# One list in place of a planner: the order of all operations in an attention kernel with a mixing and a channel stage

## The chip, the core and the metric

The kernel runs on one core of a Trainium2 chip. The metric is the device time of one execution in microseconds (us), the median of several. The core has five sequences of instructions that run side by side and wait for each other through semaphores: TensorE (PE in the profile, its weight loads apart as PEld), VectorE (DVE), ScalarE (ACT), GpSimd (POOL) and SyncE (SP), which here issues all the transfers between main memory and the core's own memory.

## What is computed

Four batches, eight heads, 768 positions, 64 numbers a head. Each position attends to a window of 16 positions either side and to 24 summaries of blocks of 32 positions (the largest key, the mean value). The attention's result x, 768 x 512 a batch, then goes through two stages:

```python
k_sum = k.reshape(B, H, nb, block, D).max(axis=3)
v_sum = v.reshape(B, H, nb, block, D).mean(axis=3)
scores_l = scale * q @ k.T, masked to |i - j| < 16
scores_s = scale * q @ k_sum.T + log(32)
a = softmax(concatenate([scores_l, scores_s]))
x = a @ concatenate([v, v_sum])              # 4 x 768 x 512
theta = x @ w_theta
zr, zi = x * cos(theta), x * sin(theta)
y = w_tok_r @ zr + w_tok_i @ zi              # 768 x 768 weights, mixing positions
u = x + y
out = u + relu(u @ w_ch)
```

Inputs and outputs are 32-bit floats. The weights arrive as pairs of 32-bit words that are turned into floats on the core.

## The kernel before

The work goes by tiles of 128 queries, 24 in all, six a batch. A tile has: scores on PE (tiles s0 and s1, L691, 32 short products), softmax on DVE (L729) and ACT (L733), transposes on PE (pa, L742), the products with v (pa, L716, here "values"), their division by the row sums (xn, L754 to L763), a turn on PE (t, L772), theta on PE (t, L797 for the first six tiles, L802 later), cosine and sine (w, L811 to L827), z (zh and zb, L837) and its split into a high and a low part (L523, L532). When a tile's z is there, one step of the mix can run on PE (m, L865): a batch has two halves of the columns with six steps each, and a step takes one tile's z and one row block of both mixing weights. The mix is over half of all time on PE. The first batch's first half works on whole floats, the rest on high and low parts (three products for one). The channel stage comes last (L906 to L1000).

Around it: SP loads q, keys (kn), v, vn, and weights (wth for theta, wt for the mix, 12 transfers wtr and wti). The block maxima of the keys are taken on DVE (ks, L614), the block means of v for the first batch on PE (pa from x, L620, x being where vn lands), the windows of the keys are copied on ACT or POOL (k, L684). A weight is turned from words to floats in five steps (f and wt, L575 to L586) and split by a cast (L525) and a subtraction (L532). Tiles named with a buffer (x, v, f, w) have between one and four buffers and a transfer waits until the buffer's last reader has ended; v has four (VB=4), two a tile.

What sets the order: all operations are first collected in a list of objects with a cost for each engine that may run them. `Program.schedule` computes due times, walks four times forward and backward through a plan of the times on every engine, and makes a last pass in which tables of numbers (OFF, HOLD and TILT, by kind and index of an operation) shift ranks, hold operations back and tilt the choice between DVE and POOL. The planner chooses the engine of each operation too. The instructions are then issued in that order, so each engine's queue, SP's among them, runs in it.

Two parts of it matter here. From the eighth tile on (FUSE=7) the values of one tile and the scores of the next are one operation, issued on PE as a row, values first (`products(scores)`, L694 to L704, L709). And a POOL operation that uses the memory port it has in common with DVE waits for the latest DVE operation that by the plan has ended before it (GATE, L1119).

Of the kernel before, what the change touches and what calls it, by code (L numbers as in the profile page):

```python
# [54 lines left out]
OFF = {  # L55
# [160 lines left out]
class Program:  # L216
# [4 lines left out]
    LANDING = 2.2  # L221
# [53 lines left out]
    def forward(self, rank, held=None):  # L275
# [7 lines left out]
        for o in self.ops:  # L283
            o.left, o.ready = o.before, held[o.seq] if held else 0.0
# [903 lines left out]
```

## Time and profile before

| | |
|---|---|
| median of the runs | 465.31 us (3 runs, 465.31 to 466.07) |
| the profiled execution | 469.32 us, of it the span 467.5 us |
| PE busy | 441.8 us, 94% of the span |
| DVE busy | 343.8 us, 74% |
| ACT busy | 286.3 us, 61% |
| POOL busy | 89.1 us, 19% |
| transfers | 55.80 MB, mean 119 GB/s |

The span runs from the first to the last instruction of the profiled execution. In a row of a timeline the idle time ahead of an instruction and what released it stand in brackets. The granted clock (PEclk) is the share of TensorE's full clock in a stretch: 1.00 is 2.4 GHz, 0.50 is 1.2 GHz.

### The profile page before, as it was taken

The page shows a single profiled execution, that of the slowest core. Times are in us where ns is not written, and L with a number is a line of the kernel's source. Part 1 is how long each engine was busy: PE and PEld are TensorE (multiplying, and loading weights), DVE is VectorE, ACT ScalarE, POOL GpSimd, SP SyncE. Part 2 cuts the span into 40 slices and gives each one's busy share as a digit, 9 for nine tenths or more (in the row PEclk, how much of TensorE's full clock was granted, in tenths as well). Part 3 has the DMA queues.
Part 4 walks back from the last instruction along what each step waited for, and adds up shares of the span by engine and source line. Part 5 has one row for each costly group of instructions (what it writes and reads, how often), then busy time and mean ns, then how long its engine had stood idle before and what let it go on. Part 6 is the DMA issues. An engine that isn't in the chain of part 4 may idle for free.

```text
span 467.5 us, 9469 instructions
## 1 busy us (share of the span) xinstructions
PE 441.8 (94%) x3552; PEld 357.7 (77%) x3552; DVE 343.8 (74%) x953; ACT 286.3 (61%) x602; POOL 89.1 (19%) x121
## 2 busy tenths in 40 slices
PE   5598699999989999999999999999999999999997
PEld 0365355566778888888888888888888878899996
DVE  2899689997964667575648667563764379999997
ACT  1799779889956479667647878573852232242531
POOL 1131231333400131121012121212000010243340
PEclk9989889999999999999999999999999999999999
DMA  7999833532445252123052321020000480013324
GB/s 289 374 318 423 214 106 133 167 108 62 125 135 184 81 170 71 52 66 103 5 195 87 96 59 58 5 89 0 2 2 1 142 309 0 1 57 112 119 101 152
DMA packets 25005, 55.80 MB, mean 119 GB/s; under 512 B 2944, under 2 KB 8320, under 8 KB 24960
## 3 DMA queue, kind: packets, MB, share of 16 engines
q1 hardware_dynamic: 24960, 55.20, 35.4%
q8 instruction: 28, 0.46, 0.4%
q14 instruction: 17, 0.14, 0.1%
HBM read 45.75 MB, written 9.44 MB: 118 GB/s over the span
## 4 chain that ended last, share of the span: by engine, by line
PE 64%; DVE 15%; DMA 13%; ACT 3%; SPq 2%; issue 1%; POOL 0%; DVEq 0%; POOLq 0%
PE m L865 29%; PE t L802 10%; PE c L981 6%; PE m L981 5%; DMA v<-vg 5%; PE pa L716 4%; PE s L691 3%; PE pa L742 3%; DMA wt<-wtr 3%; SPq L517 2%; DVE wt L532 2%; DMA x<-vn 2%; PE t L772 2%; DMA f<-vT 1%; DVE cb L906 1%
## 5 line engine op out<-in xcount | busy, mean ns | idle before, releaser
L865 PE MATMUL m<-wt,zh 128*128 128x512 f32 (+1 forms) x768 | 182.4, 362 | 0.8 <-DVE x L884 0.6
L865 PEld LDWEIGHTS m<-wt,zh 128*128 128x128 f32 x768 | 123.5, 189 | 34.0 <-issue 13.5
L865 PE MATMUL m<-wt,zl 128*128 128x512 f32 x336 | 86.8, 339 | 0.0
L733 ACT ACTIVATE e<-e,st 128x118 f32<-128x118 f32 x192 | 59.0, 383 | 2.3 <-DVE st L729 2.1
L865 PEld LDWEIGHTS m<-wt,zl 128*128 128x128 f32 x336 | 51.2, 188 | 7.4
L729 DVE CUSTOM_DVE_ANT_0 e<-s,cs 128x118 f32<-128x118 f32 x192 | 42.1, 274 | 13.1 <-PE s L691 9.1
L802 PE MATMUL t<-wth,xh 128*128 128x512 f32 x144 | 47.6, 412 | 1.1 <-DVE xl L778 1.0
L684 POOL COPY k<-kn 128x188 f32<-128x188 f32 x56 | 18.2, 356 | 108.9 <-PE s L691 72.8
L716 PEld LDWEIGHTS pa<-v,e 118*64 118x64 f32 x768 | 25.3, 141 | 14.0 <-DMA v<-vg 5.7
L746 ACT COPY e<-pa 118x512 f32<-118x512 f32 x40 | 22.8, 586 | 21.3 <-PE pa L742 21.1
L716 PE MATMUL pa<-v,e 118*64 118x65 f32 x768 | 28.8, 228 | 7.1 <-DMA v<-vg 7.1
L814 DVE TENSOR_SCALAR w<-w 128x512 f32<-128x512 f32 x17 | 7.2, 426 | 34.2 <-ACT w L811 34.2
L811 ACT ACTIVATE w<-t,bmagic 128x512 f32<-128x512 f32 x24 | 16.5, 687 | 24.8 <-PE t L802 22.4
L532 POOL TENSOR_TENSOR zl<-zb,zh 128x512 fp32r<-128x512 f32 x9 | 13.1, 1455 | 89.0 <-ACT zh L523 65.2
L691 PE MATMUL s<-k,q 64*64 64x118 f32 x768 | 26.1, 274 | 3.7 <-ACT xl L575 1.7
L733 ACT ACT_TABLE_LOAD x20 | 25.7, 1283 | 5.0 <-DVE st L729 4.7
L742 PEld LDWEIGHTS pa<-cs,e 128*118 128x118 f32 x192 | 23.0, 137 | 6.9 <-ACT e L733 1.6
L802 PE MATMUL t<-wth,xl 128*128 128x512 f32 x72 | 28.3, 393 | 0.0
L742 PE MATMUL pa<-cs,e 128*118 128x128 f32 x192 | 28.2, 275 | 0.0
L691 PEld LDWEIGHTS s<-k,q 64*64 64x64 f32 x768 | 20.5, 136 | 9.0 <-issue 3.1
L826 ACT ACT_TABLE_LOAD x21 | 26.9, 1283 | 0.4
L614 DVE TENSOR_REDUCE ks<-kn 128x48 f32<-128x1536 f32 (+1 forms) x10 | 14.3, 1432 | 15.5 <-DMA kn<-kT 15.4
(166 smaller groups left out, 776.8 us busy)
## 6 DMA issues: line engine op xcount, KB each, us to landing
v<-vg SPq DMA_DIRECT2D x48, 195.0 KB, 3.3
q<-qg SPq DMA_DIRECT2D x24, 256.0 KB, 3.2
kn<-kT SPq DMA_DIRECT2D x6, 798.0 KB, 6.2
wt<-wtr SPq DMA_DIRECT2D x6, 768.0 KB, 11.2
wt<-wti SPq DMA_DIRECT2D x6, 768.0 KB, 12.5
f<-vT SPq DMA_DIRECT2D x12, 384.0 KB, 3.4
cu<-u_scratch SPq DMA_DIRECT2D x8, 384.0 KB, 7.1
out<-cu SPq DMA_DIRECT2D x16, 192.0 KB, 1.9
```

The costliest lines, as they stand in the source:

```text
L532: lambda e: V[e].tensor_tensor(dst(), src(), hi().bitcast(F32), op=ALU.subtract), reads, writes, due, port=BOTH)
L684: lambda e, dst=dst, src=src: (nc.scalar.copy if e == "ACT" else V[e].tensor_copy)(dst(), src()), rd, [(k, key)], due, port=BOTH)
L691: scores = (0.79 if len(parts) == 1 else 2.1, [lambda p=p, g=g, h=h, c=c, kk=kk: nc.tensor.matmul(sc[h].get()[ROW[g], p, c], q.get()[ROW[h ...
L716: mm(2 * 0.433 + scores[0] + (0.2 if scores[0] else 0.0), [lambda n=n, g=g, a=a: nc.tensor.matmul(xa[a].get()[ROW[g], n], turned[a].get()[ ...
L729: op({"DVE": 0.205}, lambda eng, n=n: nc.vector.tensor_tensor_reduce(e()[:, n], sc[n % 2].get()[:, 2 * a + n // 2], mask(m), -SCALE, 3.0e3 ...
L733: op({"ACT": 0.288}, lambda eng, n=n: nc.scalar.activation(e()[:, n], e()[:, n], AF.Exp, bias=st.get()[:, n:n + 1], scale=-1.0), [(st, n)] ...
L742: mm(NH * 0.109, [lambda n=n: nc.tensor.transpose(tp.get()[:NK, n], e()[:, n], ident()) for n in range(NH)], [e_ref, (cs, "ident")], [tp], ...
L746: lambda e: (nc.scalar.copy if e == "ACT" else nc.vector.tensor_copy)(t.get()[:NK], tp.get()[:NK].rearrange("k n q -> k (n q)")), [tp], [t ...
L802: calls = [lambda t=t, xx=xx, k=k, c=c: nc.tensor.matmul(th.get(), xx.get()[:, c], w_th[c].get()[:, k], start=(c == 0 and t == 0), stop=(c ...
L826: nc.scalar.activation(w.get()[:, 0], w.get()[:, 0], AF.Sin, bias=bright.get(), scale=-1.0)
L865: nc.tensor.matmul(acc[th](), zz.get()[:, r, cc], w[:, TT[th]], start=(s == 0 and r == 0 and t == 0 and (th == 0 or c == 0)), stop=(s == N ...
L981: calls = [lambda k=k, t=t, x=x, y=y: nc.tensor.matmul(to.get(), weights[n][x][0]()[:, k, j * P:(j + 1) * P], operands[n].get()[:, y, k], ...
```

## The change

The planner goes. `schedule()` reads the order from a string, ORDER, of 2019 numbers: each is the index of an operation in the collected list, with a letter where more than one engine may run it (a ACT, d DVE, g POOL). The tables OFF, HOLD and TILT and the functions `forward` and `backward` are removed. FUSE is 99, so that no tile has its scores in one operation with the values of another. A POOL operation on the shared port waits for the operation ahead of it in the list that uses the port, if that is one of DVE's. The constants of the old plan's costs (SWITCH, LANDING, LAST, c_dma) change too, but nothing reads a time from them any more. The changed file has 227 lines fewer ahead of the kernel's own code, so L691 of before is L464 of after.

```diff
-OFF = {
-    "": {0: -75.284},
...
-HOLD = {
...
-TILT = {
...
+ORDER = """
+6 8 7 9 10 12 11 13 27g 22 29a 28a 31a 30a 32 1 33 41 42 46 34 14 0 161g 162g 66 16 4 44 45 37 35 67d 43 47 38 48 39 36 68d
...
-    LAST = (dict(PE=0, ACT=0.4283, DVE=0.7305, POOL=0.6962, SP=0), -2.5188, 6.204)
+    LAST = (dict(PE=0.0, ACT=0.42, DVE=1.2, POOL=0.95, SP=0.0), 0.0, 0.0)
...
-    def forward(self, rank, held=None):
...
+    def schedule(self):
+        order = []
+        for word in ORDER.split():
+            o = self.ops[int(word.rstrip("padg"))]
+            o.eng = dict(p="PE", a="ACT", d="DVE", g="POOL").get(word[-1]) or min(o.cost)
             order.append(o)
...
-            A1=13, T1=10, PREP=5, QB=2, VSPE=1, VB=4, KN=2, DIRECT=0, FUSE=7, GATE=1, RELOAD=2, RT=6, RM=6, XA=6, XB=2, ZB=4, ZS=6, EB=3, TAU_A=8.2, TAU_M=4,
+            A1=13, T1=10, PREP=5, QB=2, VSPE=1, VB=4, KN=2, DIRECT=0, FUSE=99, RELOAD=2, RT=6, RM=6, XA=6, XB=2, ZB=4, ZS=6, EB=3, TAU_A=8.2, TAU_M=4,
...
-            mm(*scores, due, mode="block")
+            mm(*scores, due, mode="score")
...
+            if o.eng in o.port:
+                mine = [i for i in traced[n:] if i.engine == units[o.eng]]
+                if o.eng == "POOL" and port:
+                    tc.add_manual_dep(mine[0], port.name, mybir.DependencyInfo(
                         mybir.DependencyClass.Sync, mybir.DependencyReason.DATA), reason="port")
+                port = mine[-1] if o.eng == "DVE" else None
```

What the list does is seen in the order of instructions on an engine. Three places follow; a name ends in the number of its buffer in the program, and x4 is four instructions in a row.

PE at the start of the program, before: the last scores of the first tile, the rest of the block sums of v, the first scores of the second tile (s0_190).

```order
L691 MATMUL s1_133<-k_118,q_96 64x118
L691 MATMUL s0_131<-k_118,q_96 64x118
L691 MATMUL s1_133<-k_118,q_96 64x118
L620 MATMUL pa0_98<-x_83,vt_77 24x512 x2
L691 MATMUL s0_190<-k_118,q_104 64x118
L691 MATMUL s1_192<-k_118,q_104 64x118
L691 MATMUL s0_190<-k_118,q_104 64x118
```

The same place after:

```order
L464 MATMUL s1_96<-k_86,q_88 64x118
L464 MATMUL s0_94<-k_86,q_88 64x118
L464 MATMUL s1_96<-k_86,q_88 64x118
L393 MATMUL pa0_154<-x_123,vt_125 24x512 x6
L515 MATMUL pa1_166<-cs_112,e_117 118x128 x4
L515 MATMUL pa0_182<-cs_112,e_114 118x128 x4
L464 MATMUL s0_190<-k_86,q_175 64x118
L464 MATMUL s1_192<-k_86,q_175 64x118
```

All block sums of v (four of them stood ahead of the first tile's scores) now stand between the first and the second tile's scores, together with the first tile's transposes (pa1_166 and pa0_182).

SP from the fifth weight load of the mix on, before: wt are weight loads, v_177 (the first of these) and v_169 are v of the fourth tile, v_154 is of the fifth.

```order
L517 DMA wt_337<-wtr 128x1536
L517 DMA wt_346<-wti 128x1536
L517 DMA wt_356<-wtr 128x1536
L517 DMA wt_363<-wti 128x1536
L517 DMA wt_391<-wtr 128x1536
L517 DMA wt_416<-wti 128x1536
L517 DMA wt_437<-wtr 128x1536
L517 DMA v_177<-vg 96x520
L517 DMA wt_499<-wti 128x1536
L517 DMA v_154<-vg 96x520
L517 DMA v_169<-vg 96x520
```

The same place after, where v_218 and v_222 are v of the fourth tile and v_177 is of the fifth:

```order
L290 DMA wt_294<-wtr 128x1536
L290 DMA wt_296<-wti 128x1536
L290 DMA q_454<-qg 128x512
L290 DMA v_218<-vg 96x520
L290 DMA v_177<-vg 96x520
L290 DMA v_222<-vg 96x520
L290 DMA q_477<-qg 128x512
L290 DMA wt_479<-wtr 128x1536
L290 DMA v_173<-vg 96x520
L290 DMA wt_482<-wti 128x1536
L290 DMA wt_484<-wtr 128x1536
```

The fourth tile's v now stands behind four weight loads and ahead of the other eight; before, all twelve stood ahead of its second transfer.

DVE ahead of the third tile's z (zh_815), before: conversions of weights (f and wt), w, and two reduces of the second batch's keys (ks).

```order
L614 TENSOR_REDUCE ks_731<-kn_690 128x48
L815 ISA w_711<-t_636,w_711 128x512
L581 TENSOR_SCALAR f_724<-f_724 128x768
L581 TENSOR_SCALAR f_735<-f_735 128x768
L583 SCALAR_TENSOR_TENSOR f_724<-wt_391,f_724 128x768
L583 SCALAR_TENSOR_TENSOR f_735<-wt_416,f_735 128x768
L586 SCALAR_TENSOR_TENSOR wt_808<-wt_391,f_724 128x768
L586 SCALAR_TENSOR_TENSOR wt_808<-wt_416,f_735 128x768
L837 TENSOR_TENSOR zh_815<-xn_573,w_711 128x512
L614 TENSOR_REDUCE ks_731<-kn_770 128x48
L756 RECIPROCAL st_616<-st_616 128x4
```

The same place after, where the third tile's z is zh_795:

```order
L352 TENSOR_SCALAR f_765<-f_765 128x768
L354 TENSOR_SCALAR f_763<-f_763 128x768
L354 TENSOR_SCALAR f_765<-f_765 128x768
L356 SCALAR_TENSOR_TENSOR f_763<-wt_488,f_763 128x768
L356 SCALAR_TENSOR_TENSOR f_765<-wt_490,f_765 128x768
L359 SCALAR_TENSOR_TENSOR wt_793<-wt_488,f_763 128x768
L610 TENSOR_TENSOR zh_795<-xn_518,w_661 128x512
L359 SCALAR_TENSOR_TENSOR wt_793<-wt_490,f_765 128x768
```

The reduces of the second batch's keys are now 14 and 25 rows behind this z.

Over the whole program, PE issues the same products. DVE has 27 instructions fewer, POOL 5 more and heavier ones: of the subtractions that split a mixing weight (L532 wt<-wt) seven go from DVE to POOL. ACT has 16 loads of its function tables fewer. In 18 places PE goes from one tile's scores straight to another's values; before, it went from values straight to scores in 18.

## Rows read from the trace of the kernel before

**Rows 1.** table of stretches: us; busy of PE, PEld, DVE, ACT, POOL; clock, DMA

```profile
0.00:43.40 43.40, 30.47 (x316) 16.66 (x317) 33.13 (x119) 28.91 (x73) 7.78 (x17) 0.96 0.95 345
43.40:60.00 16.60, 12.08 (x67) 7.36 (x66) 12.07 (x33) 12.79 (x34) 4.40 (x5) 0.86 0.81 241
60.00:120.00 60.00, 58.02 (x435) 35.61 (x434) 54.00 (x145) 52.42 (x115) 19.67 (x26) 0.98 0.34 111
120.00:140.00 20.00, 18.62 (x158) 15.47 (x157) 16.09 (x42) 13.72 (x28) 3.76 (x4) 1.00 0.48 152
...
360.00:467.50 107.50, 102.83 (x581) 95.73 (x580) 91.45 (x156) 34.24 (x57) 22.39 (x11) 1.00 0.31 108
```

**Rows 2.** waits of PE: us in all, times, longest us

```profile
PE pa L716 <- DMA v<-vg: 7.1, 3, 4.3
```

**Rows 3.** PE's timeline: start, us, operation, count, idle time before

```profile
5.09 6.51 PE L620 MATMUL pa<-x,vt 128*24 128x512 f32 x8 [5.09 <-DMA x<-vn]
...
25.11 1.85 PE L691 MATMUL s<-k,q 64*64 64x118 f32 x32 [1.10 <-DMA q<-qg]
...
34.76 1.04 PE L691 MATMUL s<-k,q 64*64 64x118 f32 x32
35.73 1.15 PE L716 MATMUL pa<-v,e 118*64 118x65 f32 x32
...
43.42 2.74 PE L865 MATMUL m<-wt,zh 128*128 128x512 f32 x8
...
56.67 2.00 PE L716 MATMUL pa<-v,e 118*64 118x65 f32 x32 [4.33 <-DMA v<-vg]
...
74.71 4.03 PE L865 MATMUL m<-wt,zh 128*128 128x512 f32 x12
```

**Rows 4.** one stretch of the same table, with the half clock

```profile
57.00:59.00 2.00, 2.00 (x33) 1.88 (x30) 0.47 (x3) 0.52 (x3) 0.00 (x0) 0.50 0.03 11
```

**Rows 5.** stretches, with DVE's busy time alone: clock, DMA share

```profile
22.45:42.40 19.95, 19.68 (x82) 0.91 0.99 354
42.40:73.71 31.31, 24.65 (x50) 0.89 0.69 218
```

**Rows 6.** DVE's timeline

```profile
8.28 3.91 DVE L614 TENSOR_REDUCE ks<-kn 128x24 f32<-128x768 f32 x4 [7.34 <-DMA kn<-kT]
...
57.85 0.28 DVE L729 CUSTOM_DVE_ANT_0 e<-s,cs 128x118 f32<-128x118 f32 x1 [3.29 <-PE pa L716]
...
65.37 1.75 DVE L614 TENSOR_REDUCE ks<-kn 128x48 f32<-128x1536 f32 x1 [0.64 <-DMA kn<-kT]
...
73.71 0.69 DVE L837 TENSOR_TENSOR zh<-xn,w 128x512 f32<-128x512 f32 x1 [0.77 <-ACT w L827]
```

**Rows 7.** SP's timeline: issues of transfers

```profile
40.33 4.01 SPq L517 DMA_DIRECT2D v<-vg  x3
```

**Rows 8.** chain of work that ended last: start, us, what

```profile
42.15 14.47 DMA v<-vg
...
462.13 2.10 PE c L981 x12
```

**Rows 9.** DMA issues: KB each, median us to landing

```profile
v<-vg SPq DMA_DIRECT2D x48, 195.0 KB, 3.3
...
wt<-wtr SPq DMA_DIRECT2D x6, 768.0 KB, 11.2
```

**Rows 10.** one stretch of the table, for its DMA share and GB/s

```profile
30.00:55.00 25.00, 20.96 (x187) 12.26 (x186) 23.78 (x73) 24.30 (x56) 7.01 (x8) 1.00 1.02 364
```

**Rows 11.** groups of instructions by line and form: busy, mean ns

```profile
L532 DVE TENSOR_TENSOR wt<-wt 128x768 fp32r<-128x768 f32 x8 | 7.4, 964 | 0.0
...
L532 POOL TENSOR_TENSOR wt<-wt 128x768 fp32r<-128x768 f32 x3 | 6.5, 2167 | 6.5 <-DVE wt L532 5.6 <-ACT w L820 1.0
```

**Rows 12.** timelines of POOL and DVE, one operation of each

```profile
117.20 1.29 POOL L532 TENSOR_TENSOR zl<-zb,zh 128x512 fp32r<-128x512 f32 x1 [1.42 <-ACT zh L523]
...
117.97 1.07 DVE L532 TENSOR_TENSOR zl<-zb,zh 128x512 fp32r<-128x512 f32 x1
```

More of the change, by code (lines that the diff above doesn't have):

```diff
@@ new lines @@
+944 956 892 945 927a 929a 946g 947 969 930 970 1105 894d 895d 1023a 948a 949 978 971 972 973 950 980 1021g 1106a 931a 976
+1107 979 893 1108d 952d 932 933d 1022g 953g 955 957 958 960 975 1020a 977 981 974 984 983 982 985 934a 935 997d 998d 936d
+1109 986 1110 961 1111 988 1112 959 1113 987a 989a 1024 1114d 1011d 1115 990 1052d 991a 1012g 1070a 1178 1025 1033 994d
+1179a 992 1027 995 1026 951 993d 1036 1028 1035 1181d 1180 1031 1029 1030 1001 999 1002 1000 1040 1037 1039 1032 1067g 1069g
+1068g 1009 996d 1034 1038 1003 1005 1182 1041 1183 1018 1134 1136 1019 1065 1064 1004 1043 1013 1184 1014 1185 1116a 1117
@@ new lines @@
+1647 1651 1653 1652 1654 1625 1626 1627 1648 1628d 1649d 1629g 1663 1672 1674 1673 1675 1664d 1650d 1676 1678 1665 1666d
+1667 1668 1670a 1680a 1669 1728 1729 1671g 1735 1741 1730d 1681g 1690a 1742a 1731d 1736d 1732 1737d 1738 1739 1691d 1740
+1733 1743d 1677 1679 1682 1684 1683 1687 1686 1685 1689 1692 1693 1688 1694 1771 1835 1837 1773 1747 1774 1696a 1697g 1748a
+1702a 1734 1757d 1695 1772 1838 1836 1744 1745 1749d 1750 1751 1752 1746 1753d 1775a 1776d 1758d 1765a 1766d 1754d 1703d
+1755d 1756d 1761d 1777d 1698 1700 1699 1701 1793 1759a 1708a 1714a 1794a 1769a 1762d 1770d 1760d 1706 1704 1707 1705 1712
@@ L189 @@
+1926 1930 1937 1870 1802 1898 1895 1806 1887 1810 1877 1874 1934 1834 1827 1951 1947 1958 1813 1866 2001 1988 1976d 1989
+1891 1986 1991 1992 2002a 2004a 2012 1993 1823 1955 1831 2013 2008 2009 2010 2014 2005 1990 1994 2011 2015 2006 2007 2016
+2017 2018 1995 1996 1997
+"""
 class Ref:
@@ L225 @@
               ("block", "whole"): 0.185, ("whole", "split"): -0.06, ("split", "theta"): 0.037, ("theta", "split"): 0.023,
-              ("theta", "whole"): 0.05, ("theta", "block"): 0.12, ("block", "theta"): 0.185, ("whole", "theta"): -0.06}
+              ("theta", "whole"): 0.05, ("theta", "block"): 0.12, ("block", "theta"): 0.185, ("whole", "theta"): -0.06,
+              ("block", "score"): 0.2, ("score", "block"): 0.15, ("score", "split"): 0.185, ("score", "whole"): 0.185, ("score", "theta"): 0.185,
+              ("split", "score"): 0.16, ("whole", "score"): 0.09, ("theta", "score"): 0.12}
     SAME = 0.0
@@ L397, in backward @@
-    def backward(self, span):
-        later = {o: [(u, (self.OWN if o.eng == u.eng and not o.lag else self.LAT[o.eng]) if timed else None) for u, timed in o.users]
-                 for o in self.ops}
-        for refs, _ in self.tags.values():
-            for n, r in enumerate(refs):
-                if n:
-                    later[refs[n - 1].users[0]].append((r.users[0], None))
-                if n >= r.bufs:
-                    for o in refs[n - r.bufs].users:
-                        later[o].append((r.users[0], self.LAT[o.eng]))
-        left, earlier = dict.fromkeys(self.ops, 0), {o: [] for o in self.ops}
-        for o, us in later.items():
-            left[o] = len(us)
-            for u, _ in us:
-                earlier[u].append(o)
-        now = dict.fromkeys(("PE", "ACT", "DVE", "POOL", "SP"), span)
-        ready = {o: span for o in self.ops}
-        heap = {e: [] for e in now}
-        start = {}
-        for o in self.ops:
-            if not left[o]:
-                heap[o.eng].append(o)
-        while len(start) < len(self.ops):
-            best = None
-            for e, os in heap.items():
-                for o in os:
-                    k = (min(now[e], ready[o]), o.done)
-                    if best is None or k > best[0]:
-                        best = (k, o)
-            (end, _), o = best
-            heap[o.eng].remove(o)
-            now[o.eng] = start[o] = end - o.cost[o.eng]
-            for d in earlier[o]:
-                for u, lat in later[d]:
-                    if u is o:
-                        ready[d] = min(ready[d], start[o] + (d.cost[d.eng] if lat is None else -lat - d.lag))
-                left[d] -= 1
-                if not left[d]:
-                    heap[d.eng].append(d)
-        return [start[o] for o in self.ops]
@@ L440, in schedule @@
-    def schedule(self):
-        for o in self.ops:
-            o.before = o.left
-        for o in reversed(self.ops):
-            for u, timed in o.users:
-                o.due = min(o.due, u.due - (0.15 + o.lag if timed else 0.0))
-            o.due -= min(o.cost.values())
-            o.rank += o.due
-        rank = [o.rank for o in self.ops]
-        self.spans = []
-        for n in range(self.ROUNDS):
-            span, order = self.forward(rank)
-            self.spans.append(span)
-            rank = self.backward(span)
-        self.PEN, self.KEEP, self.SAME = self.LAST
-        at = lambda table, o: table.get(o.key[0], {}).get(o.key[1], 0.0)
-        for o in self.ops:
-            o.tilt = at(TILT, o)
-        span, order = self.forward([a + at(OFF, o) for a, o in zip(rank, self.ops)], [at(HOLD, o) for o in self.ops])
-        self.spans.append(span)
+    def schedule(self):
[3 more added lines that the diff above has]
+            o.eng = dict(p="PE", a="ACT", d="DVE", g="POOL").get(word[-1]) or min(o.cost)
+            order.append(o)
+        assert len(order) == len(self.ops)
@@ L484, in c_dma @@
 def c_dma(nbytes, run=2048):
-    return nbytes / run * (7.1 + run / 26.6) * 1e-3 / 16
+    return nbytes / run * (8.4 + run / 22.5) * 1e-3 / 16
 BOTH = ("DVE", "POOL")
@@ L1110, in attn_moe @@
     with tc.manual_schedule(engines={ET.PE, ET.Activation, ET.DVE, ET.Pool, ET.SP}):
-        traced, units = nc.cur_bb.bb.instructions, dict(DVE=ET.DVE, POOL=ET.Pool)
-        shared = []
+        traced, units, port = nc.cur_bb.bb.instructions, dict(DVE=ET.DVE, POOL=ET.Pool), None
         for o in order:
@@ L1115, in attn_moe @@
             o.fn(o.eng)
-            mine = [i for i in traced[n:] if i.engine == units.get(o.eng)]
-            if o.eng == "DVE":
-                shared.append((o.done, mine[-1]))
-            elif o.eng == "POOL" and o.port and K["GATE"]:
-                begin = o.done - o.cost["POOL"]
-                ahead = [i for t, i in shared[-40:] if t + pr.LAT["DVE"] <= begin]
-                if ahead:
-                    tc.add_manual_dep(mine[0], ahead[-1].name, mybir.DependencyInfo(
+            if o.eng in o.port:
+                mine = [i for i in traced[n:] if i.engine == units[o.eng]]
+                if o.eng == "POOL" and port:
+                    tc.add_manual_dep(mine[0], port.name, mybir.DependencyInfo(
                         mybir.DependencyClass.Sync, mybir.DependencyReason.DATA), reason="port")
+                port = mine[-1] if o.eng == "DVE" else None
     es.close()
```

184 lines of the change are left out of this document (66 added, 118 removed), and 123 rows, old and new, of tables (HOLD, OFF, TILT).

## The prediction

> **What bounds the kernel now.** I read the table of stretches first. TensorE (PE) is busy in almost all of the span; what it loses lies at the two ends. Up to the first mix product at 43.4 it works 30.47 of 43.40 us, from there to 60 it works 12.08 of 16.60 at a granted clock of 0.86; from 60 to 120 it idles 1.98, from 120 to 140 1.38, in the last 107.5 us 4.67 [rows 1]. So the end is set by PE's own work plus what it loses, and 17.5 us of its idle time lie ahead of 60. A reordering can win only there; DVE, ACT and POOL work counts only where PE waits for it.
>
> The table of PE's waits names the largest in the head: the values products wait 7.1 us for v, one of these waits 4.3 [rows 2]. In PE's timeline it stands ahead of 56.67, in the middle of the first batch's mix [rows 3]; and then the products run at half clock, 0.50 granted from 57 to 59, after an idle stretch [rows 4]. Why was v late? SP issued it in the group that began at 40.33 [rows 7], behind the weight loads, and the chain shows 14.47 us of transfer from 42.15 on [rows 8]. The DMA engines were full then (share 1.02, 364 GB/s [rows 10]), and a weight load is 768 KB [rows 9], 2.1 us at that rate.
>
> The other side of the head is DVE. Between the second tile's softmax and the first z it is full: 19.68 of 19.95 us; between first and third z it works 24.65 of 31.31 [rows 5]. Of these 6.66 us of waiting 3.29 are the late values product again, seen from DVE; the rest are short ones of which a keys transfer (0.64) and w (0.77) are two [rows 6]. The third z (73.71) is what releases the third mix step at 74.71 [rows 3, 6].
>
> **The change, part by part.** The number of matrix products is the same; the order moves.
>
> *Keys first in SP's queue.* Before, constants and vn stood ahead of the keys, and the key reduces began at 8.28 after 7.34 us of waiting, taking 3.91 [rows 6]. Now the four key transfers stand first. Transfers of vn and constants that were queued ahead of the keys go behind them, so I estimate that the reduces end some 3 us earlier, at 9.2 and not 12.2, and that the first scores begin at about 10. But these scores then come first on PE and cold: the scores at 25.11, released after a wait, took 1.85 and not 1.04 [rows 3], so I take 1.9. Next in PE's order stand all block sums of v (L620, 12 instructions in the trace; eight took 6.51 [rows 3], so 9.8 at that pace and 4.9 if all of it was at half clock; I take 7.8, as they follow cold scores but warm up on the way), then the first tile's transposes (0.9), then the second tile's scores, at about 21. The first softmax comes earlier, but DVE then waits from about 18 to 22 for the second one. I take 22.0 where before had 22.45, the start of the first stretch of [rows 5].
>
> *From there to the first z.* I added up DVE's rows by the mean times of their forms: 19.8 us before between the second softmax and the first z (the trace has 19.95, so the count is good), 22.1 after, as conversions moved ahead. 22.0 + 22.1 + 0.9 for short waits is 45.0 for the first z and 46.0 for the first mix product (42.40 to 43.42 before), 2.6 later. In exchange PE has done about 3.4 us more by then: a values op (1.15 [rows 3]), a theta product of about as much, and twelve transposes.
>
> *The third z.* Between first and third z DVE has 24.0 us of work before (24.65 in the trace) and 21.2 after; the largest piece that leaves is the next batch's key reduce of 1.75 [rows 6]. Without any wait the third z would stand at 66.2. Of the 6.66 us of waits the 3.29 go if v is in time, the key wait goes with the reduce, and 2.7 are left; I keep half, 1.4. That gives 67.6, and the third mix step at 68.6, against 74.71: **6.1 us**. PE itself needs 20.4 us from first mix product to third step by the slots of its instructions (46.0 + 20.4 = 66.4), so DVE ends last there, narrowly. The work done on PE by that point is the same in both orders (49.0 us), so this is a real gain.
>
> *v of the fourth tile.* It holds the above up. Its two transfers now stand ahead of eight weight loads that stood ahead of the second one before: 8 x 768 KB at 364 GB/s is 17 us less in the queue [rows 9, 10]. The last of the two still waits in SP's queue behind a transfer for the fifth tile, whose buffer is free when the third tile's values op has ended, about 36.4 by my count of PE. Issued at 36.8, its bounds are the 3.3 us median of all v transfers [rows 9] and the 14.5 of [rows 8]; with the queue shorter by 17 us I take about the median, so 40 to 41. PE wants it at about 42.4. Behind this wait on SP stand the weight loads of steps three to six; eight of them at 2.1 us land by about 56, and DVE asks for the fifth and sixth of these at 64, so they have cover of some 8 us. Should that cover go, the price is the same DVE path, us for us.
>
> *Steps after that.* POOL takes over seven subtractions of weights (0.964 on DVE, 2.167 on POOL [rows 11]) and some casts; 16 loads of tables go from ACT. Neither engine is late after 120, where PE idles under 1% until the tail; so I count these at what PE loses to them now: at best half of the 1.98, 1.38 and 1.4 of [rows 1] (the last is 4.67 without the 3.3 that stay behind the last product, which ends at 464.2 [rows 8]), at worst as much again for new waits, since the list has longer runs of PE work in batch one. I take a gain of 0.5, bounds -1.5 and +2.5.
>
> *Scores and values as two operations.* Values and scores were one item from the eighth tile on, values first. Now PE has scores first in 18 places, values first in fewer. The only reversed pair in the trace is at 34.76: scores 0.97 to the next start, values 1.15 long [rows 3], nothing beyond the usual. I take 0; bounds 0.1 x 18 = 1.8 either way. The old pairing kept DVE waiting for both; apart, the softmax can begin one op earlier, which matters only where DVE is last.
>
> *The wait of POOL behind DVE.* A POOL operation on the shared port now waits for the DVE operation just ahead in the list, not the last by planned time. Behind it on POOL stand later z remainders and key copies; POOL is idle four fifths of the span in the middle, and a remainder is needed one mix step later. Bounds 0 and one DVE operation (0.7) per remainder that is late; I take 0.
>
> Sum: 6.1 + 0.5 = 6.6 us. The profiled execution took 469.3 (span 467.5 and 1.8 around it), so it would be 462.7; the median of the runs lies 4.0 lower, at 465.31, and as I see no reason why the gain should differ there, **458.7**.
>
> **Rivals.** (a) *DVE waits as much as before.* If something else takes the place of the late v (w from ACT, the transposes), all 6.66 stay: third z 45.0 + 21.2 + 6.7 = 72.9, third step 73.9, gain 0.8 + 0.5 = 1.3: 464.0. For it: DVE's short waits had four different causes. Against: the largest single one has a cause that moves away.
>
> (b) *The port.* At 117.20 a POOL subtraction took 1.29 and DVE's beside it, begun at 117.97, 1.07 [rows 12], where a DVE product of the same size takes 0.69 [rows 6]; so they do delay each other. If the second is stopped for the whole time of the first, seven subtractions of 2.167 cost DVE up to 15.2, less the 6.7 it no longer does: 8.5 us more on DVE. DVE has 6.0 + 3.9 us free from 60 to 140 [rows 1], which covers most of it; one to two us would reach PE: 460.2. The Trainium skill, "SBUF — State Buffer", section "Who interferes with whom", says that a DVE instruction with two SBUF inputs contends with a GpSimd one that reads SBUF, under an exclusive lock in which the second blocks fully. By that rule this rival would be the forecast; the row at 117.97 shows a delay of 0.4, not the full rest of the POOL instruction, so I give it less.
>
> (c) *The fourth tile's v is late again*, the case on the other side. If it takes 14.5 us from 36.8, it lands at 51.3; PE stands from 42.4, and pays some 2.6 for the half clock after it, as at 56.67. From there PE has 22.9 us to the third step: 51.3 + 22.9 + 2.6 = 76.8, 2.1 later than now; less 0.5: 466.9. It turns slower at a landing about 13 us after issue. Against it speak the 17 us less in the queue.
>
> (d) *Better.* The block sums run nearly all at full clock (5.7 and not 7.8) and no short wait is left: first mix at 43.9, third step at 65, gain 9.7, and 2 after it: 453.6.
>
> The change could also not do what its words say: that is the case where the transfers' new times make no difference to the order that the chip sees; it falls together with (a).
>
> **How the numbers follow.** Forecast 458.7: 0.55; (a) 464.0: 0.17; (b) 460.2: 0.08; (c) 466.9: 0.09; (d) 453.6: 0.11. The forecast's own range is 456 to 462, from the bounds of the later steps and of the short waits. The range of 8 in 10 goes from 453.0 to 465.0: it leaves out (c) and the far half of (d). A difference of 0.2% (0.93 us) is about what a measurement of this kernel can tell from no change. Faster than 464.4: forecast, (b), (d) and over half of (a), 0.84; the same: the rest of (a) and a part of (c), 0.08; slower than 466.2: 0.08.
>
> **What would show it.** Right: first scores near 10, first mix product near 46, no wait over 1 us for v ahead of the fourth tile's values, the third step near 68.6, no stretch at half clock after 30, and the same tail. Wrong: a wait for v at 42 to 51 on PE; DVE waiting over 5 us between first and third z; DVE subtractions of z over 1 us beside POOL's in 60 to 140; a first mix product after 48, as the block sums delay the second tile's softmax beyond what I took; or new waits of PE over 3 us after 120.

## The result: 458.76 us after 465.69, and the profile after

The changed kernel takes 458.76 us (median of 4 runs, 457.86 to 459.07), the kernel before beside it 465.69 (4 runs): a ratio of 0.9839, 95% interval 0.9805 to 0.9873, so 1.6% faster. In a later comparison it was 459.59 against 467.21, ratio 0.9812 (0.9760 to 0.9863). The kernel before ran beside every later experiment too, with medians of 467.27, 467.21 and 467.25 us over 70 runs; so the gain is nearer 7.6 us than the 6.9 of the first comparison. The prediction was 458.7. The number was met more closely than the steps behind it deserve; which of them held is the matter of what follows.

The table of stretches of the changed kernel, to be read beside [rows 1] (us; busy time of PE, PEld, DVE, ACT, POOL; granted clock, DMA share, GB/s):

```profile
0.00:46.00 46.00, 33.07 (x366) 19.54 (x367) 35.17 (x125) 30.71 (x77) 10.13 (x24) 1.00 0.98 309
46.00:60.00 14.00, 13.86 (x106) 8.37 (x105) 12.90 (x30) 13.61 (x35) 1.65 (x2) 1.00 0.97 385
60.00:120.00 60.00, 58.48 (x454) 37.93 (x454) 49.94 (x158) 49.34 (x114) 27.57 (x30) 1.00 0.37 108
120.00:140.00 20.00, 19.95 (x167) 17.10 (x166) 12.41 (x36) 11.16 (x29) 6.75 (x6) 1.00 0.42 133
...
360.00:456.70 96.70, 92.36 (x522) 86.72 (x520) 87.68 (x137) 30.68 (x50) 23.31 (x14) 1.00 0.26 94
```

PE idles 13.07 us ahead of 60 (17.45 before), and the granted clock is 1.00 in every stretch of the table (0.96 and 0.86 in the first two before). Busy time went down too, with the same products: 436.5 us and not 441.8.

PE's waits, longest first (us in all, times, longest), where [rows 2] had 7.1 us for v:

```profile
PE s L464 <- POOL k L457: 10.6, 2, 10.0
PE m L638 <- DVE zh L610: 1.5, 2, 1.0
PE m L638 <- DVE x L657: 1.2, 4, 0.5
PE pa L489 <- DMA v<-vg: 0.9, 1, 0.9
```

Of the first row 10.0 us are the start of the program; no other row adds up to more than 1.5. The same in PE's timeline, beside [rows 3]:

```profile
10.03 1.85 PE L464 MATMUL s<-k,q 64*64 64x118 f32 x32 [10.03 <-POOL k L457]
11.81 6.20 PE L393 MATMUL pa<-x,vt 128*24 128x512 f32 x12
...
19.27 1.04 PE L464 MATMUL s<-k,q 64*64 64x118 f32 x32
...
41.42 1.15 PE L489 MATMUL pa<-v,e 118*64 118x65 f32 x30 [0.94 <-DMA v<-vg]
...
44.79 1.45 PE L638 MATMUL m<-wt,zh 128*128 128x512 f32 x4
...
66.07 4.14 PE L638 MATMUL m<-wt,zh 128*128 128x512 f32 x12 [0.50 <-DVE zh L610]
```

First scores at 10.03, the block sums of v behind them, the second tile's scores at 19.27, a wait of 0.94 for the fourth tile's v, the first mix product at 44.79 and the third step at 66.07, which waits 0.50 for DVE. DVE's timeline, beside [rows 6]:

```profile
7.56 2.01 DVE L387 TENSOR_REDUCE ks<-kn 128x24 f32<-128x768 f32 x2 [1.78 <-DMA kn<-kT]
...
20.49 0.28 DVE L502 CUSTOM_DVE_ANT_0 e<-s,cs 128x118 f32<-128x118 f32 x1 [0.31 <-PE s L464]
...
42.85 0.68 DVE L610 TENSOR_TENSOR zh<-xn,w 128x512 f32<-128x512 f32 x1
...
65.33 0.68 DVE L610 TENSOR_TENSOR zh<-xn,w 128x512 f32<-128x512 f32 x1
```

The key reduces end at 9.57, the second softmax begins at 20.49, the first z at 42.85, the third at 65.33. These times move from one execution to the next. A second profile of the changed kernel has, on PE and on DVE:

```profile
11.79 7.48 PE L393 MATMUL pa<-x,vt 128*24 128x512 f32 x12
...
67.47 4.14 PE L638 MATMUL m<-wt,zh 128*128 128x512 f32 x12 [0.54 <-DVE zh L610]
```

```profile
44.11 0.68 DVE L610 TENSOR_TENSOR zh<-xn,w 128x512 f32<-128x512 f32 x1
```

### The profile page after: what moved, and what is told of

It is laid out like the page before. It is cut to its first block, busy times and chain, and to the rows that moved or that the text cites. A ratio compares the mean times of both kernels' runs of the same rounds, so it can differ in the third digit from the quotient of the medians.

```text
span 456.7 us, 9383 instructions
## 1 busy us (share of the span) xinstructions
PE 436.5 (96%) x3552; PEld 355.6 (78%) x3552; DVE 336.3 (74%) x926; ACT 270.8 (59%) x608; POOL 103.0 (23%) x126
## 4 chain that ended last, share of the span: by engine, by line
PE 58%; DVE 12%; issue 1%; ACT 0%; DVEq 0%
PE m L638 31%; PE t L575 9%; PE m L754 4%; PE c L754 4%; PE pa L489 3%; DVE wt L305 3%; PE s L464 3%; PE pa L515 2%; DVE cb L679 2%; PE t L545 2%; DVE x L657 1%; DVE cu L773 1%; PE t L754 1%; DVE zl L305 1%; DVE wth L305 1%
## 5 line engine op out<-in xcount | busy, mean ns | idle before, releaser
L506 ACT ACTIVATE e<-e,st 128x118 f32<-128x118 f32 x192 | 64.0, 388 | 22.7 <-DVE st L502 21.9
L502 DVE CUSTOM_DVE_ANT_0 e<-s,cs 128x118 f32<-128x118 f32 x192 | 45.3, 273 | 4.8 <-PE s L464 4.2
L464 PE MATMUL s<-k,q 64*64 64x118 f32 x768 | 25.9, 273 | 10.7 <-POOL k L457 10.6
L584 ACT ACTIVATE w<-t,bmagic 128x512 f32<-128x512 f32 x24 | 16.5, 686 | 32.2 <-PE t L575 21.4
L464 PEld LDWEIGHTS s<-k,q 64*64 64x64 f32 x768 | 20.4, 136 | 16.5 <-POOL k L457 10.7
L610 DVE TENSOR_TENSOR w<-xn,w 128x512 f32<-128x512 f32 x18 | 12.3, 686 | 20.0 <-ACT w L600 19.9
L457 POOL COPY k<-kn 128x188 f32<-128x188 f32 x40 | 13.0, 347 | 59.9 <-DVE st L529 17.0
L588 DVE CUSTOM_DVE_ANT_0 w<-t,w 128x512 f32<-128x512 f32 x24 | 16.5, 688 | 13.2 <-POOL w L587 12.8
L657 DVE TENSOR_TENSOR x<-m,x 128x512 f32<-128x512 f32 (+1 forms) x32 | 16.3, 549 | 12.7 <-PE m L638 12.7
L575 PEld LDWEIGHTS t<-wth,xh 128*128 128x128 f32 x144 | 22.0, 189 | 2.6 <-DVE xl L551 0.4
L305 POOL TENSOR_TENSOR zl<-zb,zh 128x512 fp32r<-128x512 f32 x9 | 11.8, 1309 | 51.9 <-DVE vs L418 16.5
```

The source lines that it names most:

```text
L305: lambda e: V[e].tensor_tensor(dst(), src(), hi().bitcast(F32), op=ALU.subtract), reads, writes, due, port=BOTH)
L464: scores = (0.79 if len(parts) == 1 else 2.1, [lambda p=p, g=g, h=h, c=c, kk=kk: nc.tensor.matmul(sc[h].get()[ROW[g], p, c], q.get()[ROW[h ...
L502: op({"DVE": 0.205}, lambda eng, n=n: nc.vector.tensor_tensor_reduce(e()[:, n], sc[n % 2].get()[:, 2 * a + n // 2], mask(m), -SCALE, 3.0e3 ...
L506: op({"ACT": 0.288}, lambda eng, n=n: nc.scalar.activation(e()[:, n], e()[:, n], AF.Exp, bias=st.get()[:, n:n + 1], scale=-1.0), [(st, n)] ...
L575: calls = [lambda t=t, xx=xx, k=k, c=c: nc.tensor.matmul(th.get(), xx.get()[:, c], w_th[c].get()[:, k], start=(c == 0 and t == 0), stop=(c ...
L584: op({"ACT": 0.59}, lambda e: nc.scalar.activation(r(), th.get(), AF.Identity, bias=bmagic.get(), scale=1.0 / TWO_PI), [th, bmagic], [R], due)
```

## The experiments

In all experiments but the first the order is written as a list, as in the changed kernel, and only the list is edited; a number is an operation, a letter its engine. Differences in us are taken to the second median of the changed kernel, 459.59; ratios are to the kernel before, run beside each.

### The kernel before a second time, and its order as a list

> The kernel before, unchanged, for a second profile. The profiled execution of before was 4.0 us above the median, and the change's profiled execution is 10.9 us below it while the medians differ by 6.9. Theory A (the late v of the fourth tile and the half clock after it are there in every execution): the second profile shows again a wait of about 4 us for v at 52 to 57 and 0.50 granted after it, and the third mix step near 74.7. Theory B (the late v is a matter of one execution): a wait under 2 us, no half clock from 57 to 62, the third mix step near 71, and the 4 us of difference between profile and median are found there.

Median 468.6 beside 467.27 for the other runs of before, ratio 1.0018 (0.9983 to 1.0052). Its profiled execution took 465.26 (span 463.5). Three lines of its PE timeline:

```profile
23.17 1.78 PE L716 MATMUL pa<-v,e 118*64 118x65 f32 x32 [2.00 <-ACT e L746]
25.58 2.00 PE L691 MATMUL s<-k,q 64*64 64x118 f32 x32 [0.63 <-ACT st L754]
...
71.86 4.03 PE L865 MATMUL m<-wt,zh 128*128 128x512 f32 x12
```

and of its table of stretches:

```profile
24.00:26.00 2.00, 1.37 (x27) 1.21 (x28) 2.00 (x16) 2.00 (x9) 0.91 (x2) 0.50 0.39 131
26.00:28.00 2.00, 2.00 (x35) 1.70 (x31) 2.00 (x6) 2.00 (x8) 0.98 (x1) 0.50 1.01 268
```

The longest wait for v is 2.4 us here and not 4.3, no half clock follows it, and the third step stands at 71.86, 2.85 ahead of [rows 3]. Theory B is right on this execution, but for a wait of 2.4 where it said under 2: of the 4.0 us between the two profiles, 2.85 are there. But against the later medians near 467.2 the first profiled execution lies 2 us above and this one 2 us below. And the late v comes again: a later run, the old list with scores first, has the same order up to the third step, and its PE timeline shows

```profile
57.70 2.00 PE L489 MATMUL pa<-v,e 118*64 118x65 f32 x32 [3.91 <-DMA v<-vg]
...
75.93 4.03 PE L638 MATMUL m<-wt,zh 128*128 128x512 f32 x12
```

with a granted clock of 0.50 from 57 to 61. So a wait near 4 us is there in some executions of the old order and not in others. Half clock there is here all the same, but earlier: from 14 to 16, and from 24 to 30, after 4 us in which PE worked for 2.0 (the wait of 2.00 ahead of 23.17 is one for the eviction of the transposes).

> The changed program with the old order written out as its list: every engine has the instructions of before in the order of before, and only the waits of POOL on the shared port follow the new rule. Theory A (order alone decides): as before, 465.3, between 464.4 and 466.3. Rival (the new port rule itself gives or costs): under 463 or over 468.

```diff
 ORDER = """
-6 8 7 9 10 12 11 13 27g 22 29a 28a ...
+3 0 5 4 14 1 16 6 8 10 12 66 ...
```

Median 468.36, ratio 1.0018 (0.9987 to 1.0049): in us that is above theory A's range and past the rival's 468, but the kernel before beside it was above that range too (467.27), and by the ratio theory A holds. The profiled execution took 465.21, 3.2 us under its median, and the third step stands at 70.62. The new rule of the port does something: POOL's three subtractions of mixing weights take 1825 ns each and not 2167, and POOL is busy for 80.2 us and not 89.1. But no time comes of it that can be measured; what counts is the order.

These profiles give the account on which the rest is built (us; the last column is span less third step):

| profile | span | PE idle | third step at | from there to the end |
|---|---|---|---|---|
| before | 467.5 | 25.71 | 74.71 | 392.8 |
| before, again | 463.5 | 22.52 | 71.86 | 391.6 |
| old order as a list | 463.4 | 24.63 | 70.62 | 392.8 |
| after | 456.7 | 20.23 | 66.07 | 390.6 |
| after, again | 458.4 | 20.77 | 67.47 | 390.9 |

Ahead of the third step PE has done the same products in all of them. The means of the three and of the two: the span falls by 7.2 us, of which 5.6 are there at the third step and 1.6 come later. Split the other way, 3.8 us are less waiting of PE and the other 3.5 are the same products in less time.

More profiles share these heads. The old head of the next section has the third step at 71.17 and the old list with scores first at 75.93; the new head with either seam has it at 65.42 and 65.64. With these there are five profiles of the old head and four of the new one: as means the third step comes at 72.86 and 66.15, 6.7 us earlier. The first z stands at 43.1 and 43.3, so the lead is made behind it, between first and third z: there the old order takes 26.9 to 31.3 us with 24.3 to 24.7 of work on DVE, the new one 21.2 to 22.6 with 21.2 to 21.4.

### Half of one order, half of the other

> The first 450 of the 2019 operations as in the new list (up to the mix steps of the first half of batch one, some 75 us), all others in the order of before. Theory A (the gain is made ahead of the third mix step): 459.5, at most 1.5 us above the changed kernel. Rival C (the gain is made by the rest: values and scores apart, subtractions on POOL, fewer table loads): 464 to 466. The seam itself may cost up to 1.5 us.

```diff
 ORDER = """
 6 8 7 9 10 12 ... 560 509a 692d
-388g 449g 511g 460 ...
+690g 511a 512a 510a ...
```

> The reverse: the first 448 operations as before, the others in the order of the new list. Theory A: 464.5 to 466.5. Rival C: 459 to 460. If both parts give half each, this and the kernel with the new head both stand at 462.

```diff
 ORDER = """
-6 8 7 9 10 12 ...
+3 0 5 4 14 1 ... 436 496 387
...
```

Both missed their ranges: new head 466.92, ratio 0.9991 (0.9964 to 1.0018); old head 467.23, ratio 0.9991 (0.9962 to 1.0020). For the old head the ratio is what theory A said: its third step is at 71.17 and 392.0 us follow, so the new order of the rest gives nothing behind the old head. For the new head it is not: the third step is at 65.42, as early as in the changed kernel, and then 398.3 us follow. So the early third step is the head's work, but in this kernel nothing of it is left at the end. PE's timeline of the kernel with the new head shows where it is lost:

```profile
65.42 4.14 PE L638 MATMUL m<-wt,zh 128*128 128x512 f32 x12 [0.50 <-DVE zh L610]
...
93.43 0.62 PE L515 MATMUL pa<-cs,e 128*118 128x128 f32 x4 [3.41 <-ACT e L506]
...
104.56 0.66 PE L545 MATMUL t<-cs,xn 128*128 128x128 f32 x4 [1.09 <-DVE w L588]
```

The transposes at 93.43 wait 3.41 us for an exponential on ACT; from 60 to 140 PE idles 6.77 us (1.6 in the changed kernel), with a clock of 0.98.

> As the kernel with the new head, but the seam is put at operation 950, about a third into the program, where the two orders have done nearly the same (12 operations differ; 26 at the earlier seam). The earlier one had the third mix step at 65.4 (before: 71.9) and lost it again: PE idles 6.3 us between 60 and 120. Theory A1 (a matter of the seam: the old order hands DVE and ACT work to a stretch that the new head has not prepared): gain kept, ratio to before 0.984 to 0.988, PE idle under 2 from 60 to 120. Rival C1 (the old order of the rest needs the time anyway, and the gain is lost later): ratio 0.995 to 1.000, with the idle time behind the seam.

```diff
 ORDER = """
 6 8 7 9 10 12 ... 929a 946g 947
-969 930 970 1105 ...
+1134 1135 1136 1137 ...
```

464.65 us, ratio 0.9932 (0.9897 to 0.9968), between the two theories. PE idles 1.68 us from 60 to 140, so the loss there was the earlier seam's; a new one stands behind the new seam:

```profile
189.93 1.65 PE L638 MATMUL m<-wt,zh 128*128 128x512 f32 x4 [3.49 <-DVE zh L298]
```

A mix step waits 3.49 us for the high part of z, and the clock is 0.99 over 140 to 360. From 360 to the end PE idles 5.28, in the changed kernel 4.34. The two kernels with the new head stand 7.3 and 5.1 us above the changed kernel; with the later seam the gain of the head is no longer given back ahead of it. How much of the 7.3 and 5.1 is the seam's and how much the old order of the rest needs anyway, these runs don't settle.

> The changed kernel, unchanged, for a second profile and a ratio to before on the same chip as the next three. Ratio to before 0.984 (0.980 to 0.988). In the profile the third mix step near 66 and no stretch at half clock after 12.

459.59, ratio 0.9812 (0.9760 to 0.9863), third step at 67.47 and not 66, no half clock in the table of stretches.

### The transfers: keys first, v of the fourth tile

> The changed kernel with the head of SP's queue as before: constants and two transfers of vn ahead of the keys. PE's order stays, so the first scores still come first. Theory A (DVE is the chain of the head): reduces end near 12.2 and not 9.6, first scores near 13, and most of the 2.6 us stays until the third mix step: 1.5 to 2.6 us slower than the changed kernel, ratio 0.986 to 0.990. Rival (DVE waits for theta's weights at 16 to 19 anyway and catches up): under 1 us slower, ratio 0.981 to 0.985.

```diff
 ORDER = """
-6 8 7 9 10 12 11 13 27g ...
+0 14 1 16 6 8 7 9 10 12 ...
```

462.73 us, ratio 0.9889 (0.9810 to 0.9968): 3.1 slower than the changed kernel, a little over theory A's range. The intervals of the two ratios overlap, but the runs don't: 461.52 to 463.02 here, 458.75 to 460.61 there. Lines of PE's and of DVE's timeline:

```profile
13.56 1.85 PE L464 MATMUL s<-k,q 64*64 64x118 f32 x32 [13.56 <-POOL k L457]
...
69.50 4.14 PE L638 MATMUL m<-wt,zh 128*128 128x512 f32 x12 [0.59 <-DVE zh L610]
```

```profile
9.17 3.93 DVE L387 TENSOR_REDUCE ks<-kn 128x24 f32<-128x768 f32 x4 [9.17 <-DMA kn<-kT]
...
47.62 0.68 DVE L610 TENSOR_TENSOR zh<-xn,w 128x512 f32<-128x512 f32 x1
...
68.77 0.68 DVE L610 TENSOR_TENSOR zh<-xn,w 128x512 f32<-128x512 f32 x1
```

The reduces end at 13.10 and not 9.57, and the first z is 4.8 and 3.5 us later than in the two profiles of the changed kernel. Between first and third z DVE takes 21.15 here and is busy for all of it, so that it catches up 1.3 to 1.5 us: the third step is 3.4 and 2.0 us later.

> The changed kernel with one transfer moved: the second of the fourth tile's v goes behind the eight weight loads that it had been put ahead of. It would be issued near 45 and land near 54 behind 17 us of weight loads; PE wants it at 40.1. Theory A (the order on SP carries the head): PE waits 10 to 14 us for v, runs at half clock after it, third mix step at 77 to 81 (66 to 67 in the changed kernel), 10 to 13 us slower than the changed kernel, ratio to before 1.005 to 1.012. Rival (the wait is made up for by DVE and ACT, which catch up on conversions meanwhile): under 5 us slower, ratio under 0.994.

```diff
 ORDER = """
...
-234 320 264 389 88 319 89 90 91 92 93 271 102 94 99 105 103
+234 320 389 88 319 89 90 91 92 93 271 102 94 99 105 264 103
```

476.88 us, ratio 1.0204 (1.0135 to 1.0273): 17 us slower, more than theory A's 10 to 13. SP's and PE's timeline and the table of stretches:

```profile
45.23 0.33 SPq L290 DMA_DIRECT2D v<-vg  x1
```

```profile
59.36 2.00 PE L489 MATMUL pa<-v,e 118*64 118x65 f32 x30 [18.24 <-DMA v<-vg]
...
83.00 6.74 PE L638 MATMUL m<-wt,zh 128*128 128x512 f32 x20
```

```profile
59.00:61.00 2.00, 1.64 (x29) 1.64 (x30) 0.00 (x0) 0.00 (x0) 0.00 (x0) 0.50 0.03 8
```

Issued at 45.23, landed at 59.3: 14 us, as in [rows 8]. PE waits 18.24 us and comes back at half clock. The last twelve of the twenty products from 83.00 on are the third step; they begin at about 85.6 by the pace of the row (theory A: 77 to 81), 18 to 20 us later than in the changed kernel. The place of one transfer of 195 KB in a queue is worth more than the whole change.

> The old order as a list, with one thing moved: the two transfers of the fourth tile's v go ahead of three weight loads (those of the fifth step's second and the sixth step's weights) and are issued near 31 and not at 36 and 40. Theory D (the late v costs what its wait shows, and what is late next on PE is only little behind): the wait of 2.2 us for v goes, the third mix step comes 1.5 to 2.5 us earlier than 70.6 to 71.9, ratio to before 0.995 to 0.997. Rival E (DVE or ACT ends last there anyway): the wait goes or becomes one for the transposes' eviction on ACT, the third mix step stays within 0.7 us, ratio 0.999 to 1.001.

```diff
 ORDER = """
...
-214 77 689a 186 92 218 215 690g
+214 77 689a 186 92 263 264 218 215 690g
...
-232 199 264 269
+232 199 269
...
-325 108 263 244 111d
+325 108 244 111d
```

465.80 us, ratio 0.9962 (0.9932 to 0.9992). PE's timeline, of the list of the old order and then of this kernel, and a line of this kernel's DVE:

```profile
54.83 1.15 PE L489 MATMUL pa<-v,e 118*64 118x65 f32 x32 [2.17 <-DMA v<-vg]
...
70.62 4.03 PE L638 MATMUL m<-wt,zh 128*128 128x512 f32 x12
```

```profile
65.03 0.66 PE L545 MATMUL t<-cs,xn 128*128 128x128 f32 x4 [2.20 <-DVE w L588]
...
71.87 4.03 PE L638 MATMUL m<-wt,zh 128*128 128x512 f32 x12
```

```profile
62.63 1.75 DVE L387 TENSOR_REDUCE ks<-kn 128x48 f32<-128x1536 f32 x1 [1.40 <-DMA kn<-kT]
```

The wait for v (2.17) is gone; but the turn of a later tile now waits 2.20 for w, and the third step doesn't come earlier than in the profile of the unmoved list, as rival E said. DVE holds it: in both profiles it waits for the second batch's keys (1.40 us here, 1.16 there) and reduces them, with w behind that, and its third z stands at 69.31 and 69.68. By the time, though, theory D was right: the ratio lies in its range and its interval just excludes 1. The median is 2.6 us under that of the unmoved list, with intervals that overlap by little. The two findings fit if what goes is the later v of the longer executions, since the profile of the unmoved list lies 3.2 us under its median; that isn't shown. In the old order v was one of two things that came late together; the other, the reduce of the next keys, is what the new list has moved behind the third z.

### Scores ahead of values, or behind

> The changed kernel, but in the 18 places where PE goes from one tile's scores straight to another tile's values the values come first, as before. Theory F (the split is worth nothing by itself): as the changed kernel, ratio to before 0.982 to 0.987. Rival G (scores first let the softmax begin a products op, some 1.1 us, earlier where DVE ends last): 1.5 to 4 us slower than the changed kernel, ratio 0.988 to 0.993, with PE waiting in those places.

```diff
 ORDER = """
...
-371g 601 608 654a 561 642a 547 553 549 562 588 589a 649
+371g 601 561 642a 547 553 549 562 588 608 654a 589a 649
...
```

466.31 us, ratio 0.9971 (0.9946 to 0.9995): 6.7 slower than the changed kernel. Neither theory gave so much. The pair itself costs the same in either order: from the start of the first to the start of what follows, 2.06 us as a mean over 15 pairs behind 70 in each profile of the changed kernel and over 14 in this one. The waits of PE that are new or longer:

```profile
PE pa L489 <- ACT e L519: 2.5, 7, 0.7
PE s L464 <- DVE st L502: 1.7, 1, 1.7
PE t L575 <- DVE xl L551: 1.6, 4, 0.7
```

Seven times the values come before ACT has evicted the transposes that they read, time that the scores had filled. Three of the 18 places lie ahead of 70, and the first is not as before: there the second tile's scores stood ahead of the first tile's values in the old order too. Here they come behind them, and the second softmax begins 1.4 to 2.6 us later than in the changed kernel:

```profile
23.11 0.28 DVE L502 CUSTOM_DVE_ANT_0 e<-s,cs 128x118 f32<-128x118 f32 x1 [2.68 <-PE s L464]
```

With the waits in the first 30 us the half clock is back:

```profile
24.00:26.00 2.00, 1.35 (x26) 1.28 (x29) 1.79 (x13) 2.00 (x9) 0.61 (x1) 0.76 1.03 395
26.00:28.00 2.00, 2.00 (x21) 1.70 (x14) 1.24 (x3) 0.86 (x4) 0.61 (x1) 0.50 1.00 391
```

PE's idle time is 25.09 us, 4.6 over the two profiles of the changed kernel, and its busy time 3.1 over.

> The old order as a list, with one thing changed: in the 17 places where values and the next tile's scores stood as one operation, the scores come first. So it is that part of the change alone. The opposite swap in the new list cost 6.7 us, about half of it in the first 50 us and half in waits of values for the transposes' eviction. Theory F (the order of a pair is worth something only in a list that was arranged around it; the old order loses 0.2 us from 140 to 360 and has nothing to give): ratio 0.998 to 1.004. Rival G (scores first is better as such): 2 us faster or more, ratio under 0.996.

```diff
 ORDER = """
...
-771a 556d 773a 588 608 550 772
+771a 556d 773a 608 588 550 772
...
```

467.67 us, ratio 1.0024 (0.9991 to 1.0057): nothing, as theory F said. Scores first are worth 0 in the old order, and values first cost 6.7 in the new one, part of it in the first tiles, where the old order didn't have values first in this way. The pair has no price of its own; what it costs depends on the arrangement around it.

### POOL's subtractions

> The changed kernel with eight subtractions that split mixing weights back from POOL to DVE (the eight of which before did them there). Theory A (DVE is not last where they stand, and the port is no matter): within 1 us of the changed kernel, ratio 0.981 to 0.987. Rival H (DVE is last from 60 to 140, and the 7.7 us that it is spared there count): 3 to 6 us slower, ratio 0.990 to 0.996. Rival B (the shared port: DVE is held while POOL subtracts): faster by 1 us or more.

```diff
 ORDER = """
...
-694g ... 259g ... 261g ... 317g ... 371g ... 373g ... 442g ... 501g
+694d ... 259d ... 261d ... 317d ... 371d ... 373d ... 442d ... 501d
```

Seven of the eight split a mixing weight; 694 splits a weight of theta. 470.17 us, ratio 1.0056 (1.0019 to 1.0093): 10.6 slower, far outside every theory. The third step is at 66.09, as in the changed kernel; most of the loss is in one place, in the timelines of PE, DVE and POOL:

```profile
123.33 1.19 PE L575 MATMUL t<-wth,xh 128*128 128x512 f32 x2 [7.45 <-DVE xl L551]
```

```profile
116.77 2.54 DVE L305 TENSOR_TENSOR wt<-wt 128x768 fp32r<-128x768 f32 x1 [1.69 <-POOL wt L298]
120.24 1.54 DVE L305 TENSOR_TENSOR wt<-wt 128x768 fp32r<-128x768 f32 x1 [0.92 <-POOL wt L298]
```

```profile
115.91 0.83 POOL L298 CAST wt<-wt 128x768 fp32r<-128x768 f32 x1
116.70 1.80 POOL L305 TENSOR_TENSOR wt<-wt 128x768 fp32r<-128x768 f32 x1
```

A subtraction stands on DVE where its cast on POOL is not yet done: DVE waits 1.69 us. It then begins 0.07 us after POOL's own subtraction and takes 2.54 where it takes 0.95 by itself. The next one does much the same (0.92 of waiting, 1.54 us), beside a cast on POOL. Behind the two, in DVE's queue, stands the low part of x for theta (xl, L551), and PE waits 7.45 us for that. DVE is busy 7.40 us of 10 from 110 to 120, the held time counted as busy: it is not full, it is blocked in its order. After the wait PE's clock is 0.69 from 120 to 130.

## Why the prediction was right, point by point

- **The place of the gain: right.** 5.6 of 7.2 us are there at the third mix step, 6.7 over all profiles with either head. Predicted were 6.1 and 0.5 behind it; the latter is 1.6, inside its bounds. That the lead lasts to the end is the list's as a whole: with the old rest behind it, it was lost.
- **The base of the sum: 2 us too late, and hidden.** The 6.1 was taken against 74.71, which one execution showed [rows 3]; five profiles of the old head have 70.62 to 75.93, 72.86 as a mean. The third step was forecast at 68.6 and came at 66.07 and 67.47. In the terms of the sum: the first z was put 2.6 us later than before and the stretch from first to third z 8.7 shorter; as means they came 0.2 later and 6.7 shorter. Two misses of 2 us and more nearly cancelled, and that is luck.
- **Keys first: mechanism right, times too late.** Reduces to 9.57 (9.2 predicted), scores at 10.03 (10) in 1.85 us (1.9). The block sums took 6.20 in the first profile and 7.48 in the second (7.8 predicted), the second softmax began at 20.49 and 21.75 (22.0), the first z stood at 42.85 and 44.11 (45.0). So the block sums vary by over 1 us from one execution to the next, and the forecast fits the second. From the second softmax to the first z it was 22.36 in both, with 21.78 of work in the first, not 22.1 + 0.9. Put back, the old head of the queue costs 3.1 us.
- **First to third z: right.** 22.5 us (42.85 to 65.33) for 21.2 + 1.4; the kernel with the keys late shows the 21.15 without waits. In the old order this stretch takes 27 to 31. DVE's lighter share, 24.3 to 24.7 against 21.3, is some 3.2 us of the difference; the rest are its waits, 2.6 to 3.0 us in three of the old profiles and 6.5 to 6.7 in the two with the latest v, against 1.2. DVE does end last: the third step waits 0.50 for it. No run takes this work off DVE by itself; the account is by the profiles.
- **v of the fourth tile: in time, as said** (0.94 us of waiting in the first profile, none in the second). Moved by itself in the old order, it gives 1.4 us against before (ratio 0.9962) and 2.6 against the unmoved list, of the 3.29 that the prediction had for it. Rival (c) had the right mechanism and price: from the landing of v to the third step its sum gives 22.9 + 2.6 = 25.5 us, and the run with v late took 26.2 (59.36 to about 85.6) and was 17 us slower.
- **The clock: seen, not counted.** The prediction named "no stretch at half clock after 30" as a sign, which held, and priced half clock in rival (c) alone. Of the 7.2 us some 3.5 are the same products in less time. The granted clock was 0.50 in the old order from 25 to 28 and 56 to 62 (before), 14 to 16 and 24 to 30 (again), and 23 to 26 (as a list). These 3.5 are not a gain beside the 5.6, but the same time counted by another split. The half clock ahead of the first z costs that z little: it stands at 42.4 and 42.8 with some 3 us of half clock ahead of it (before, as a list) and at 43.3 with some 10 (again). Where half clock follows the late v, the third z is late with it: 31.3 and 31.0 us behind the first and not 27 to 28.
- **Scores and values: 0, right for the pair** (2.06 us either way). Not foreseen was that the new list needs the order of its pairs: 6.7 us.
- **POOL's subtractions: 0 predicted.** On POOL they took 1.83 us each, not 2.167. What stands behind them was not looked at; back on DVE, in this list, they cost 10.6 us, most of it by blocking its queue.
- **Rival (b), the port: misread.** The prediction took 117.97 for a partial delay [rows 12]. POOL's subtraction ended at 118.49, DVE's at 119.04, so DVE was held for the 0.52 that POOL still ran, and then worked 0.55: the full rest. The row at 116.77 above says it more plainly: 2.54 us, of which 1.73 until POOL's end at 118.50. So the rule cited from the Trainium skill, "SBUF — State Buffer", section "Who interferes with whom", agrees with both rows. It cost little here for another reason: from 60 to 140 of the changed kernel one subtraction on DVE is held, for 0.35 us (at 125.23), and the longest of z takes 0.73, so the sign that was named for this rival is not there.

## What to carry to other kernels

Take a term's base from more than one execution where it hangs on a transfer: the order's gain was read off a wait that varied by 2 us from one execution to the next, with half clock after it or not. A list that was arranged as a whole has no parts of a price of their own: an exchange that is worth nothing in one list costs 6.7 us in the other, and half of one list before half of the other gained nothing in two runs and 0.7% in a third. Look at what is queued behind an instruction before moving it to another engine's queue: in the run with the subtractions on DVE the price was the wait of PE for an instruction behind them, 7.45 us, not their own 0.95.

## What the runs showed of the hardware

- DVE's subtraction with two operands in the core's memory, begun 0.07 us after one of POOL's, took 2.54 us for 0.95: it was held for 1.73 until POOL had ended, and the hold shows as a longer duration, not as a wait before it. What was left after POOL's end took 0.81 for 0.95 (at 116.77 and 120.24) and 0.55 for 0.69 (at 117.97 of before), 0.14 less than the instruction by itself.
- In the run with v late PE did nothing from 41.1 to 59.4; the granted clock was 0.50 from 46 on and stayed there for the first 7 us of work, up to 66.4. In the second profile of before 4 us with 2.0 of work (20 to 24) were followed by 6 us at 0.50.
- At the start of the program the granted clock reads 1.00, and yet the changed kernel's first scores took 1.85 us, as long as the scores at 25.11 of before at a granted clock of 0.50; the same scores take 1.04 later on.
- A transfer of 195 KB took 14.1 us from issue to landing behind eight of 768 KB in the run with v late, and 6.4 ahead of them in the changed kernel (issued at 35.0, landed at 41.4).
